# Splitting the last q,k products among the scores, shifting the first block's transposed scores, and respacing the mixer weights and the last row blocks

## The chip, the cores and the metric

The kernel runs on one core of a Trainium2 chip. The metric is the device time of one execution in microseconds (us), as the median of several runs. All matrix work is on TensorE (PE in the profile; PEld is its weight load). VectorE is DVE, ScalarE is ACT, GpSimd is POOL, and SP is the engine whose queue issues most transfers. A `q` behind an engine's name in a row (SPq, ACTq) means its instruction queue, for instance when it issues a DMA.

## The reference

One transformer-like block over S = 2048 rows of D = 576 numbers. A condition vector gives six modulation vectors (scale, shift and gate of two halves).

```
x = A_x
h = layernorm(x) * (1 + ca) + sa
x = x + ga * attention(h)      # 32 heads of 18, causal, window of 256 keys, output projection wo
h = layernorm(x) * (1 + cb) + sb
x = x + gb * mixer(h)          # token shift between gelu(layernorm(h) @ w1) and @ w2,
                               # then an MLP 576 -> 4608 -> 576 (w3, w4), both with residuals
```

All products are carried out to nearly full precision: each operand is split into a high part, rounded to the matmul type, and the rest (low part), and three products (high x high, low x high, high x low) are summed. So a product over 576 = 4 x 128 + 64 input numbers takes 4 x 3 + 2 = 14 matmuls.

## The kernel before, in words

**Phase A** (`phase_a`, L127) does the first half of the block, and its stages overlap:

- *Products.* The rows come in four groups of 512 (g = 0 to 3). `vproj` (L394) makes v; `qproj(m, g)` (L413) makes the m-th set of 128 of the 1152 rows of transposed q and k for group g: 14 matmuls of 128x512 (L422) into one PSUM bank, a high part by ACT (L424), a low part by DVE (L425), and two stores to DRAM (`qkh`, `qkl`, L427), issued on ACT's queue. The PSUM bank comes from `dense` (L387), which takes tag "sc" and tag "st" in turn; each tag has three banks. The order of the products is the list `jobs`; its last seven are (m, g) = (8,1), (7,2), (3,2), (8,2), (7,3), (3,3), (8,3).
- *Attention units.* There are 32 units, each for one group of 512 queries and four heads: n = 0 to 7 belong to g = 0 (the first block, with fewer keys), 8 to 15 to g = 1, and so on. A unit's operands are loaded into one of four buffers U (`uload`, L444; the transfers are at L451), which reuse the memory of the products' inputs and weights. In `s2` (L464) PE makes 16 score tiles (L477, tag "sc"), and DVE takes each one's row maximum (L484), which also frees the bank. The maxima, negated and split (L490, L491), are transposed by PE (`mT`, L498, tag "tr"), copied by ACT (`ms`, L500) and written into the operand U by a DMA (L501, "the ms store"). Then `s3` (L505) makes the scores again, transposed and with the maximum subtracted by the matmul (X, L526, plus a mask by L527, tag "st", three banks), ACT takes the exponential (P, L533), PE multiplies with v (`av`, L548), ACT copies the result (L553), PE transposes it back (`oT`, L560, tag "tr"), DVE divides (L562, L566), and every second unit SP stores the rows (`od`, L570).
- *Row blocks.* For each 128 rows `s4` (L734) loads attention's rows (`or`) and x (`xr`), transposes and splits them (`split9`, L64: PE L68 and L72, ACT L69 and L73, DVE L70 and L74), multiplies with `wo` in two halves (L761) and adds (L762), stores xp, and then normalizes twice in place, each time with a store (L99, L101, the store hbd; L884, the store xnd). L99 overwrites what the store of xp reads. Row blocks 0 to 11 are done in phase A beside the next block's units, 12 to 15 at the start of the next phase.
- *Weights of the mixer.* At the end of phase A `load_w1` (L785) loads w1 in ten pieces (SP, L803 and L77, L78) through two raw buffers, splits them by ACT (L825, L826) and DVE (L827, L829), and `load_w2` (L833) does the same for w2 (SP L842, ACT L857, DVE L858).

**Phase B and C** (`phase_bc`, L869) do the mixer: transposes of the normalized rows (`xnT`, L1055, split by ACT L911 and DVE L912), w1 (L957), w2 (L1010), and the MLP (L1116 and L1145).

**What sets the order.** Each step has a due time in units (one attention unit is 1.0), and `play` (L40) issues steps in order of due time. Phase A is built under a setting that fixes this order on PE, POOL and SP; on ACT and DVE, and in the later phases, the framework's scheduler orders the instructions itself. A product has 3.25/12.5 = 0.26 units. The products end at `t_end`, and the first score is due 1.55 units ahead of that (`u0`), so the last six products lie among scores. A unit that starts at tb has its 16 scores from tb to tb + 0.95 (each maximum is listed a little behind its score), mT at tb + 1.15, X from tb + 1.5 (`o3`) to tb + 2.5, oT at tb + 2.72 and its store at tb + 2.82. The due times of a row block are the seven numbers of `d5`: load, transposes, first half, second half, first and second statistics, and the delay of a store behind the step before it:

```
d5 = (-1.1, 0.0, 0.3, 0.5, 1.3, 2.3, 0.55)
```

Of the kernel before, what the change touches and what calls it, by code (L numbers as in the profile page):

```python
# [8 lines left out]
F32 = mybir.dt.float32  # L9
# [10 lines left out]
P = 128  # L20
# [30 lines left out]
class Kern:  # L51
# [75 lines left out]
    def phase_a(self):  # L127
        nc = self.nc
# [10 lines left out]
        with ExitStack() as st:  # L139
# [86 lines left out]
            def warm(k):  # L226
                def f():
                    pw = self.ps.tile([P, 512], F32, tag="sc", name=f"pw{k}", bufs=self.b_sc)
                    for _ in range(self.n_warm[k]):
                        nc.tensor.matmul(pw, self.zb, self.zb.unsqueeze(1).to_broadcast([P, 4, P]), start=True, stop=True)  # L230
                return f
# [155 lines left out]
            def dense(shape, name):  # L387
                tag, nb = banks_p[turn[0] % len(banks_p)]
                turn[0] += 1
                return self.ps.tile(shape, F32, tag=tag, name=name, bufs=nb)  # L390
# [19 lines left out]
                    nc.scalar.copy(dst, pv.rearrange("p (h d) -> p h d", d=DH))  # L410
                return f

            def qproj(m, g):  # L413
                def f():
                    L, w = hT[g], Wq[m]
                    pq = dense([P, 512], f"pq{m}_{g}")
                    pl = []
                    for k in range(KC):
                        pl += [(w[:, k, :], L[:, k, :]), (w[:, KC + 1 + k, :], L[:, k, :]), (w[:, k, :], L[:, KC + k, :])]
                    pl += [(w[:, KC, :], L[:, 2 * KC, :]), (w[:, 2 * KC + 1, :], L[:, 2 * KC, :])]  # L420
                    for n, (a, b) in enumerate(pl):
                        nc.tensor.matmul(pq, a, b, start=(n == 0), stop=(n == len(pl) - 1))  # L422
                    hl = pp.tile([P, 2, 512], F32R, tag="P", name=f"hl{m}_{g}", bufs=self.b_p)
                    nc.scalar.copy(hl[:, 0, :], pq)  # L424
                    nc.vector.tensor_tensor(out=hl[:, 1, :], in0=pq, in1=hl[:, 0, :].bitcast(F32), op=ALU.subtract)  # L425
                    for n, dst in enumerate((qkh, qkl)):
                        nc.scalar.dma_start(dst[m * P:(m + 1) * P, g * 512:(g + 1) * 512], hl[:, n, :].bitcast(F32))  # L427
                return f
# [194 lines left out]
            s4 = self.s4  # L623

            def sub2(c, g, hq, tb):
                st, f1, f2 = s2(c, g, hq)
                return [(tb + 0.95 * t / 16, f) for t, f in st] + [(tb + 0.96 + 0.06 * self.lt, f1), (tb + 1.05 + self.l_m, f2)]

            def sub3(c, g, hq, tb):
                st, n, f1, f2, f3 = s3(c, g, hq)  # L630
                e = max(t for t, _ in st) / n * self.ww
                return [(tb + self.ww * t / n, f) for t, f in st] + [(tb + e + self.l_f, f1), (tb + e + self.l_f + self.l_o, f2), (tb + e + self.l_f + self.l_o + self.l_s, f3)]

            UN = 12.5
            dv, dq = 1.9 / UN, 3.25 / UN
            T0 = -16.2
            ev = [(T0 - 1.99, lambda: lns[0][0]()), (T0 - 1.98, consts), (T0 - 1.975, cond), (T0 - 1.97, warm(0))]
# [10 lines left out]
            jobs = []  # L648
# [10 lines left out]
                jobs += [("q", m, g) for m in late]  # L659
            T = T0  # L660
            first, last = {}, {}
            for kind, a, b in jobs:
                g = a // 4 if kind == "v" else b
                key = ("v", b) if kind == "v" else ("q", a)
                first.setdefault(("h", g), T)
                first.setdefault(key, T)
                last[key] = T
                if kind == "v":
                    if g == b == 0:
                        ev += [(T0 + 0.001 * (4 * n + a), vproj(a, b, n)) for n in range(3)]  # L670
                    else:
                        ev.append((T, vproj(a, b)))
                    T += dv
                else:
                    ev.append((T, qproj(a, b)))
                    T += dq
            self.t_end = T
            for t in range(4, NT):
                g, i = divmod(t, 4)
                ld, stt, nm, tr = lns[t]  # L680
# [16 lines left out]
            shift = self.t_end + self.u0  # L697

            n = 0
            for g in range(NGA):  # L700
                for c in range(NCH):
                    for hq in range(2):
                        tb = n + shift
                        tu = tb - self.u_ld
                        ev.append((max(tu, ta[n] + 0.01) if n < 4 else tu, uload(c, g, hq)))
                        ev.append((tb - 0.001, lambda c=c, g=g, hq=hq, tb=tb: sub2(c, g, hq, tb)))
                        ev.append((tb + self.o3 - 0.001, lambda c=c, g=g, hq=hq, tb=tb + self.o3: sub3(c, g, hq, tb)))
                        n += 1
                for i in range(4 if g < 3 else 0):
                    t4 = n - 1 + shift + self.o3 + self.ww + self.l_f + self.l_o + self.l_s + self.l_r + 2.0 * i - self.d5[0]  # L710
                    ev += [(t4 + d, f) for d, f in s4(g, i, self.d5)]
            uw = shift + 2.0
            wb, steps = woload()
            ev.append((uw, wb))
# [2 lines left out]
            for v in (2, 3, 4, 5):  # L717
                steps, spill, store = modvec(v)
                t0 = T0 + self.t_mv + self.d_mv * (v - 2)
                for k, (ld, ch) in enumerate(steps):  # L720
                    ev += [(t0 + 0.3 * k, ld), (t0 + 0.3 * k + 0.5, ch)]
                ev += [(t0 + 2.0, spill), (t0 + 2.1, store)]
            tw = n - 0.1 + shift
            wb, steps = self.load_w1()
            ev.append((tw, wb))
            w2 = self.load_w2()
            for n, (ld, f) in enumerate(steps + w2):
                d = 0.17 if n < len(steps) else 0.08
                t0 = tw + 0.17 * min(n, 10) + 0.08 * max(0, n - 10)
                ev += [(t0 + 0.01 if n < 18 else t0 + 1.4 * d - 0.005, ld), (t0 + 1.4 * d, f)]  # L730
            with self.tc.manual_schedule(engines=self.manual):
                play(ev)

# [445 lines left out]
    u0, u_ld = -1.55, 1.3  # L1179
    e_ld, e_tr, e_w2, e_x1, e_lt, e_s4 = 1.2, 0.7, 1.2, 0.8, 0.8, 0.0  # L1180
    d4 = (-0.2, 0.1, 0.38, 0.56, 0.85, 1.2, 0.02)
    d5 = (-1.1, 0.0, 0.3, 0.5, 1.3, 2.3, 0.55)
    l_r = 0.5
    t_mv, d_mv = 3.6, 2.3
# [9 lines left out]
    o3, ww = 1.5, 1.0  # L1194
# [27 lines left out]
```

## Time and profile before

| | before |
|---|---|
| median of three runs | 1772.54 us (1772.39 to 1774.01) |
| the profiled execution | 1772.65 us |
| its span, first to last instruction | 1770.4 us |
| PE busy | 1722.6 us (97%) |
| DVE, ACT, POOL busy | 976.2, 594.3, 389.7 us |
| mean granted TensorE clock | 0.993 |

The profiled execution's time is 2.25 us more than its span. Times in rows are counted from the span's start. In the trace the first score starts at 200.59 us, the last q,k product's matmuls at 222.83, attention's last transposes at 662.64, and the first matmul of w1 at 671.87.

A row of a timeline has the start, the length, the engine, the line, the operation, the tile that it writes and those it reads, the shape and the number of merged instructions; in brackets stands how long the engine was idle before it, and what ended the idle time. A row of the waits has who waited for whom, the sum in us, how often, and the longest.

### The profile page before, as it was taken

The page shows a single profiled execution, that of the slowest core. Times are in us where ns is not written, and L with a number is a line of the kernel's source. Part 1 is how long each engine was busy: PE and PEld are TensorE (multiplying, and loading weights), DVE is VectorE, ACT ScalarE, POOL GpSimd, SP SyncE. Part 2 cuts the span into 40 slices and gives each one's busy share as a digit, 9 for nine tenths or more (in the row PEclk, how much of TensorE's full clock was granted, in tenths as well). Part 3 has the DMA queues.
Part 4 walks back from the last instruction along what each step waited for, and adds up shares of the span by engine and source line. Part 5 has one row for each costly group of instructions (what it writes and reads, how often), then busy time and mean ns, then how long its engine had stood idle before and what let it go on. Part 6 is the DMA issues. An engine that isn't in the chain of part 4 may idle for free.

```text
span 1770.4 us, 30143 instructions
## 1 busy us (share of the span) xinstructions
PE 1722.6 (97%) x11700; PEld 1493.0 (84%) x11700; DVE 976.2 (55%) x2674; ACT 594.3 (34%) x1262; POOL 389.7 (22%) x379
## 2 busy tenths in 40 slices
PE   7999999999999989999999999999999999999999
PEld 5898766777777768899899999999999999999998
DVE  5412378788888866977544444444444444444434
ACT  4622156655555565344211111111111111111111
POOL 4543431000000000211342333224431121122100
PEclk8999999999999999999999999999999999999999
DMA  6536654444544436622211111111110000000002
GB/s 177 148 110 208 200 161 124 117 147 121 153 126 147 129 111 191 201 81 89 63 56 36 49 42 56 34 36 56 56 36 29 16 29 14 29 29 29 1 1 107
DMA packets 97712, 156.89 MB, mean 89 GB/s; under 512 B 11034, under 2 KB 40478, under 8 KB 97570
## 3 DMA queue, kind: packets, MB, share of 16 engines
q1 hardware_dynamic: 86612, 135.12, 25.5%
q10 hardware_dynamic: 10958, 19.85, 3.2%
q8 instruction: 93, 1.52, 0.4%
q14 instruction: 49, 0.40, 0.1%
HBM read 107.06 MB, written 47.20 MB: 87 GB/s over the span
## 4 chain that ended last, share of the span: by engine, by line
PE 55%; DVE 2%; POOL 1%; issue 0%; DMA 0%; SPq 0%; ACT 0%; ACTq 0%; DVEq 0%; POOLq 0%
PE p L1145 26%; PE p L1116 22%; PE p L1118 2%; PE p L1117 2%; PE w L1010 2%; PE pg L957 2%; DVE x L1011 0%; DVE G L975 0%; DVE G L962 0%; DVE LNT L70 0%; DMA r<-in_B_w_dram 0%; POOL CW L1100 0%; DVE xm L884 0%; DVE CW L1095 0%; DVE Gc L1127 0%
## 5 line engine op out<-in xcount | busy, mean ns | idle before, releaser
L1145 PEld LDWEIGHTS p<-CW,Gc 128*128 128x128 f32 x3456 | 473.8, 188 | 16.2 <-DVE Gc L1127 3.7
L1145 PE MATMUL p<-CW,Gc 128*128 128x288 f32 x3456 | 482.0, 295 | 3.4 <-DVE Gc L1127 3.4
L1116 PE MATMUL p<-LNT,CW 128*128 128x512 f32 x1728 | 419.1, 391 | 0.0
L1116 PEld LDWEIGHTS p<-LNT,CW 128*128 128x128 f32 x1728 | 316.3, 188 | 58.8
L1124 ACT ACTIVATE gfc<-p 128x512 f32<-128x512 f32 x144 | 86.2, 599 | 735.6 <-PE p L1118 735.6
L1149 DVE TENSOR_TENSOR acc<-p,acc 128x288 f32<-128x288 f32 x340 | 154.1, 456 | 319.6 <-PE p L1145 316.2
L484 DVE CUSTOM_DVE_ANT_0 sc<-sc,mask 128x384 f32<-128x384 f32 (+2 forms) x512 | 260.5, 556 | 65.9 <-PE sc L477 63.2
L533 ACT ACTIVATE P<-X 128x384 f32<-128x384 f32 x480 | 221.6, 490 | 121.5 <-PE X L527 108.3
L477 PE MATMUL sc<-U 126*128 126x384 f32 (+2 forms) x512 | 195.3, 403 | 7.3 <-DVE m L484 5.6
L526 PE MATMUL X<-U 128*128 128x384 f32 (+2 forms) x704 | 180.8, 316 | 5.9 <-DMA U<-ms 3.2
L1149 DVE TENSOR_TENSOR accw<-p,accw 128x288 f32<-128x288 f32 x204 | 90.0, 453 | 128.5 <-PE p L1145 127.3
L526 PEld LDWEIGHTS X<-U 128*128 128x128 f32 x704 | 127.2, 193 | 34.6 <-issue 24.5
L527 PE MATMUL X<-maskb,identb 128*128 128x256 bf16 x480 | 136.6, 285 | 0.0
L1127 DVE TENSOR_TENSOR Gc<-gfc,Gc 128x512 fp32r<-128x512 f32 x144 | 124.6, 866 | 4.6
L422 PE MATMUL pq<-hT,Wq 128*128 128x512 f32 x504 | 121.3, 397 | 2.4 <-POOL Wq L380 1.6
L422 PEld LDWEIGHTS pq<-hT,Wq 128*128 128x128 f32 x504 | 93.9, 188 | 24.8 <-POOL Wq L380 1.9
L477 PEld LDWEIGHTS sc<-U 126*128 126x128 f32 x512 | 97.7, 197 | 14.3 <-DVE m L484 10.9
L1096 POOL TENSOR_TENSOR CW<-r,CW 128x1024 fp32r<-128x1024 f32 x17 | 41.4, 2436 | 281.7 <-DVE CW L1094 281.7
L548 PE MATMUL av<-P,V 128*32 128x256 f32 (+2 forms) x1472 | 92.4, 381 | 0.0
L1126 ACT CAST Gc<-gfc 128x512 fp32r<-128x512 f32 x144 | 89.5, 622 | 4.6
L1100 POOL TENSOR_TENSOR CW<-r,CW 128x1152 fp32r<-128x1152 f32 x17 | 46.5, 2734 | 157.7 <-DVE CW L1099 157.7
L527 PEld LDWEIGHTS <-identb 128*128 128x128 bf16 x480 | 46.2, 96 | 36.9 <-issue 20.7
(1056 smaller groups left out, 1959.3 us busy)
## 6 DMA issues: line engine op xcount, KB each, us to landing
U<-qkh SPq DMA_DIRECT2D x156, 72.0 KB
U<-qkh SPq DMA_DIRECT2D x96, 108.0 KB
r<-in_B_w_dram SPq DMA_DIRECT2D x18, 576.0 KB
qkh<-hl ACTq DMA_DIRECT2D x36, 256.0 KB
qkl<-hl ACTq DMA_DIRECT2D x36, 256.0 KB
r<-in_B_w_dram SPq DMA_DIRECT2D x18, 512.0 KB
U<-qkl SPq DMA_DIRECT2D x78, 72.0 KB
U<-qkl SPq DMA_DIRECT2D x48, 108.0 KB
```

The costliest lines, as they stand in the source:

```text
L422: nc.tensor.matmul(pq, a, b, start=(n == 0), stop=(n == len(pl) - 1))
L477: nc.tensor.matmul(sc[:, lo:], QZ[:KR, q, i * P:(i + 1) * P], KZ[:KR, j, i * P + lo:(i + 3) * P], start=True, stop=True)
L484: nc.vector.tensor_tensor_reduce(out=sc[:, lo:], in0=sc[:, lo:], in1=mask[:, lo:], scale=1.0, scalar=-3e38, op0=ALU.add, op1=ALU.max, accu ...
L526: nc.tensor.matmul(X[:, x0:x0 + nb, :].rearrange("p a b -> p (a b)"), KZ[:, j, kb * P:(kb + 1) * P], QZ[:, q, qb * P:(qb + nb) * P], start ...
L527: nc.tensor.matmul(X[:, 0::2, :], self.identb, mk, start=False, stop=True)
L533: nc.scalar.activation(Pb[b][:, q, :], Xb[b, q].rearrange("p a b -> p (a b)"), AF.Exp, scale=SCALE)
L548: nc.tensor.matmul(abox[0][32 * q:32 * q + 32, q0:q0 + w], V[4 * g + kb][:, hv:hv + 32], Pb[b][:, q, p0:p0 + w], start=(first and n == 0), ...
L1116: nc.tensor.matmul(pg, W3[:, ws, fs], L[:, xs, :], start=(i == 0), stop=False)
L1126: nc.scalar.copy(Gh, gf)
L1127: nc.vector.tensor_tensor(out=Gl, in0=gf, in1=Gh.bitcast(F32), op=ALU.subtract)
L1145: nc.tensor.matmul(po, a, w, start=(i == 0), stop=(i == len(seq) - 1))
L1149: nc.vector.tensor_tensor(out=acc[t][:, cs], in0=po, in1=acc[t][:, cs], op=ALU.add)
```

## The change

It has four parts.

- The last seven q,k products are each issued in four pieces of 4, 4, 3 and 3 matmuls, 0.065 units apart, instead of one run of 14. Scores that are due in between are issued between the pieces. These products take their bank from tag "st" alone.
- For the units of the first block (g = 0), the transposes of the maxima (mT) and all of `s3` come 0.1 units later. The row blocks of that group keep their times.
- The load of the mixer's weights begins at 30.8 units behind the first score instead of 31.9. The pieces of w1 follow each other by 0.26 units instead of 0.17, and each is split 0.5 units behind its load instead of 0.24; for w2 it is 0.1 instead of 0.08, and 0.19 instead of 0.11.
- Row blocks 8 to 11 (g = 2) are 2.3 units apart instead of 2.0, except the last one: 0.9 units are taken off it, which puts its transposes and projection where they were. Its later steps come sooner (`d6`): its first statistics 0.75 units behind its transposes instead of 1.3, its second 1.1 instead of 2.3, and its stores 0.05 instead of 0.55 behind the step before.

```diff
-            def qproj(m, g):
+            pqs = {}
+
+            def qproj(m, g, part=None):
                 def f():
                     L, w = hT[g], Wq[m]
-                    pq = dense([P, 512], f"pq{m}_{g}")
+                    if part is None:
+                        pq = dense([P, 512], f"pq{m}_{g}")
+                    elif part == 0:
+                        pq = pqs[m, g] = self.ps.tile([P, 512], F32, tag="st", name=f"pq{m}_{g}", bufs=self.b_st)
+                    else:
+                        pq = pqs[m, g]
...
-                    for n, (a, b) in enumerate(pl):
-                        nc.tensor.matmul(pq, a, b, start=(n == 0), stop=(n == len(pl) - 1))
+                    own = range(len(pl)) if part is None else range(*self.q_parts[part:part + 2])
+                    for n in own:
+                        nc.tensor.matmul(pq, *pl[n], start=(n == 0), stop=(n == len(pl) - 1))
+                    if own[-1] < len(pl) - 1:
+                        return
...
-                return [(tb + 0.95 * t / 16, f) for t, f in st] + [(tb + 0.96 + 0.06 * self.lt, f1), (tb + 1.05 + self.l_m, f2)]
+                return [(tb + 0.95 * t / 16, f) for t, f in st] + [(tb + 0.96 + 0.06 * self.lt, f1), (tb + 1.05 + self.l_m + (0 if g else self.l_g0), f2)]
...
-                    ev.append((T, qproj(a, b)))
+                    if len(parts) < self.n_split and (kind, a, b) in jobs[-self.n_split:]:
+                        parts.append(T)
+                        ev += [(T + dq * n / 4, qproj(a, b, n)) for n in range(4)]
+                    else:
+                        ev.append((T, qproj(a, b)))
                     T += dq
...
-                        ev.append((tb + self.o3 - 0.001, lambda c=c, g=g, hq=hq, tb=tb + self.o3: sub3(c, g, hq, tb)))
+                        o3 = self.o3 + (0 if g else self.l_g0)
+                        ev.append((tb + o3 - 0.001, lambda c=c, g=g, hq=hq, tb=tb + o3: sub3(c, g, hq, tb)))
...
-                    t4 = n - 1 + shift + self.o3 + self.ww + self.l_f + self.l_o + self.l_s + self.l_r + 2.0 * i - self.d5[0]
-                    ev += [(t4 + d, f) for d, f in s4(g, i, self.d5)]
+                    t4 = n - 1 + shift + self.o3 + self.ww + self.l_f + self.l_o + self.l_s + self.l_r + (2.0, 2.0, 2.3)[g] * i - self.d5[0] - (0.9 if (g, i) == (2, 3) else 0)
+                    ev += [(t4 + d, f) for d, f in s4(g, i, self.d6 if (g, i) == (2, 3) else self.d5)]
...
-            tw = n - 0.1 + shift
+            tw = n - 1.2 + shift
...
-                d = 0.17 if n < len(steps) else 0.08
-                t0 = tw + 0.17 * min(n, 10) + 0.08 * max(0, n - 10)
-                ev += [(t0 + 0.01 if n < 18 else t0 + 1.4 * d - 0.005, ld), (t0 + 1.4 * d, f)]
+                t0 = tw + 0.26 * min(n, 10) + 0.1 * max(0, n - 10)
+                lag = 0.5 if n < 10 else 0.19
+                ev += [(t0 + 0.01 if n < 18 else t0 + lag - 0.005, ld), (t0 + lag, f)]
...
+    l_g0 = 0.1
+    q_parts, n_split = (0, 4, 8, 11, 14), 7
+    d6 = (-1.1, 0.0, 0.3, 0.5, 0.75, 1.1, 0.05)
```

More of the change, by code (lines that the diff above doesn't have):

```diff
@@ L661, in phase_a @@
             first, last = {}, {}
+            parts = []
             for kind, a, b in jobs:
```

## The prediction

> **What bounds the kernel now.** I read the page first, then busy time by stage, then what TensorE (PE) waited for in each stage, and last the timelines of the two places that the change touches.
>
> ```profile
> span 1770.4 us, 30143 instructions
> PE 1722.6 (97%) x11700; PEld 1493.0 (84%) x11700; DVE 976.2 (55%) x2674; ACT 594.3 (34%) x1262; POOL 389.7 (22%) x379
> ...
> 195.00:227.00 32.00, 28.16 (x123) 21.17 (x121) 14.65 (x56) 5.17 (x9) 6.97 (x5) 1.00 0.55 175
> 227.00:310.00 83.00, 77.76 (x725) 55.81 (x729) 67.54 (x292) 51.05 (x111) 19.97 (x17) 1.00 0.49 143
> 310.00:640.00 330.00, 323.35 (x2899) 244.99 (x2890) 272.81 (x954) 195.29 (x432) 15.86 (x40) 1.00 0.44 131
> 640.00:680.00 40.00, 32.98 (x251) 25.28 (x242) 19.89 (x61) 24.31 (x65) 2.78 (x6) 0.83 0.56 172
> 680.00:870.00 190.00, 180.21 (x1364) 173.48 (x1363) 146.21 (x424) 74.61 (x195) 41.38 (x59) 1.00 0.40 127
> 870.00:1770.00 900.00, 896.71 (x5354) 816.77 (x5352) 391.60 (x756) 170.74 (x280) 208.38 (x108) 1.00 0.12 36
> ```
>
> Each stage row gives its length, then busy time of PE, weight load, DVE, ACT and POOL, granted clock, DMA share and GB/s. PE is busy 97% of the span and is the bound everywhere. The change adds and removes no matmul; it only moves work, so it can pay only in PE's idle time and in time at a lowered clock. The execution took 1772.65 us, 2.25 more than its span and 0.11 over the median of 1772.54; I sum against 1772.65. A measurement of this kernel can tell about 0.2%, or 3.5 us, from no change.
>
> Idle are 3.8 us in 195:227 (the last q,k products among the first scores), 5.2 in 227:310 (first query block), 7.0 in 640:680 (attention's end into the next phase), the last also at a mean clock of 0.83. After 870 PE is never short of work, so what is gained ahead of it should reach the end unless a transfer on the way is late.
>
> **The split q,k products.** What PE waited for in 195:227, then the start of the mixture:
>
> ```profile
> PE sc L477 <- DVE m L484: 2.2, 5, 0.5
> PE pq L422 <- DVE m L484: 0.7, 1, 0.7
> PE sc L477 <- issue: 0.4, 1, 0.4
> PE sc L477 <- DVE hl L425: 0.2, 1, 0.2
> ...
> 195.74 0.27 ACTq L451 DMA_DIRECT2D U<-qkl  x1
> 197.23 3.53 PE L422 MATMUL pq<-hT,Wq 128*128 128x512 f32 x14
> 200.59 0.22 PE L477 MATMUL sc<-U 126*128 126x128 f32 x1
> 201.27 0.33 PE L477 MATMUL sc<-U 126*128 126x128 f32 x1 [0.45 <-DVE m L484]
> ...
> 200.86 0.30 DVE L484 CUSTOM_DVE_ANT_0 sc<-sc,mask 128x128 f32<-128x128 f32 x1 [3.20 <-PE sc L477]
> 211.41 0.57 DVE L484 CUSTOM_DVE_ANT_0 sc<-sc,mask 128x384 f32<-128x384 f32 x1 [2.35 <-PE sc L477]
> ```
>
> A product is 14 matmuls in one run of 3.53 us, so 0.25 each; then a handful of scores comes at once, and the next one waits for DVE's maximum to free a score buffer. In pieces of 4, 4, 3 and 3 there is one score (sometimes two) behind each 0.75 to 1.0 us of products. One maximum takes DVE 0.30 us for 128 columns and 0.57 for 384 (last two rows), so it is done before the next score. The products also leave the score banks for the other three ("st"). So the 2.2 + 0.7 + 0.4 + 0.2 = 3.5 us can go.
>
> Against it: the first score is now behind four matmuls of its neighbour instead of 14, ten matmuls or 2.5 us earlier, at about 198.2. The last load of its operands is issued at 195.74, on ACT's queue. Its landing isn't shown; the nearest row is unit 2's ms store, issued at 243.98 (below), for which PE stops waiting 4.2 us later. By that the load lands at 199.9 and the first score waits 1.7 us; at half that latency it waits nothing. Term: -3.5 + 0.7 = -2.8, bounds -3.5 to -1.8. The ring of three "st" banks replaces six banks: a product has two products' time, about 9 us with their scores, to be evacuated, and no row above names a wait for "st"; cost 0. If ACT fell behind by a product, PE would wait up to that product's 3.5 us.
>
> ```profile
> 234.45 0.64 ACTq L501 DMA_DIRECT2D U<-ms  x1
> 243.98 0.62 ACTq L501 DMA_DIRECT2D U<-ms  x1
> 248.17 0.41 PE L526 MATMUL X<-U 128*128 128x256 f32 x2 [1.33 <-DMA U<-ms]
> ...
> PE mT L498 <- DVE o L566: 1.9, 3, 0.9
> PE X L526 <- DMA U<-ms: 1.7, 2, 1.3
> PE mT L498 <- DVE mr L491: 1.3, 2, 0.7
> ```
>
> **First block 0.1 unit later.** The two stores lie a unit apart, 9.5 us, so 0.1 unit is about 1 us. The last three rows are the waits of 227:310. The transposes of the maxima (mT) wait 1.9 + 1.3 = 3.2 us for DVE. Both mT and the transposed scores X move, so mT stands behind one or two more scores and meets the short, 128-column maxima of the next unit instead of the long ones. Of the 3.2 us, 0.9 is the first unit of the second block, which isn't moved; there the room between oT and mT shrinks by 0.1 unit, at two units. I take -1.5 of the 2.3; bounds -2.3 to +2.0 (two units 1 us each). The distance from mT to X stays 0.35 unit, so the 1.7 us for the ms store stay; 0, bounds -1.7 to +1.
>
> **The end of attention.** PE's waits in 640:680, then stretches of 5 us, then the rows around the longest:
>
> ```profile
> PE X L526 <- ACT P L533: 2.1, 3, 1.6
> PE xnT1pa L1055 <- DVE T L912: 1.8, 1, 1.8
> PE X L526 <- DMA U<-ms: 1.4, 1, 1.4
> ...
> 645.00:650.00 5.00, 3.56 (x33) 2.44 (x26) 3.42 (x10) 3.60 (x10) 0.58 (x2) 0.95 0.51 194
> 650.00:655.00 5.00, 3.37 (x19) 2.65 (x22) 1.90 (x9) 2.12 (x7) 0.51 (x1) 0.50 0.32 86
> 655.00:660.00 5.00, 5.00 (x50) 3.25 (x45) 0.99 (x6) 3.74 (x13) 0.00 (x0) 0.86 0.36 110
> 670.00:675.00 5.00, 4.45 (x19) 3.97 (x20) 2.91 (x9) 2.37 (x7) 0.00 (x0) 0.50 0.92 275
> 675.00:680.00 5.00, 5.00 (x38) 4.96 (x37) 1.93 (x5) 3.81 (x8) 0.00 (x0) 0.81 0.76 250
> ...
> 633.48 1.83 PE L761 MATMUL po<-Wom,oT 128*128 128x288 f32 x12
> 647.65 0.47 PE L526 MATMUL X<-U 128*128 128x128 f32 x2 [1.44 <-DMA U<-ms]
> 653.40 0.69 PE L526 MATMUL X<-U 128*128 128x256 f32 x2 [1.63 <-ACT P L533]
> ...
> 646.41 0.82 DVE L99 SCALAR_TENSOR_TENSOR xr<-xr,b10mv,cb 128x576 f32<-128x576 f32 x1 [4.13 <-DMA xp<-xr]
> 649.81 4.06 SPq L803 DMA_DIRECT2D rw<-in_B_w_dram  x3
> 652.41 0.40 ACT L825 CAST W1m<-rw 128x256 fp32r<-128x256 f32 x1 [2.43 <-DMA rw<-in_B_w_dram]
> 643.68 1.64 ACT L533 ACTIVATE P<-X 128x384 f32<-128x384 f32 x4 [0.31 <-ACT P L533]
> ...
>   DMA rw<-in_B_w_dram: 5.3, 6
> ```
>
> The last unit's X waits 1.44 us for its ms store: no scores are left to fill the time behind mT. In units from the first score, row block 10's transposes move from 31.42 to 27.42 + 2 x 2.3 = 32.02, so its first half of the output projection falls at 32.32, between the last mT (31 + 1.15) and X (31 + 1.5). It is at least 1.83 us of PE work, paid elsewhere before. Term -1.4.
>
> Then a chain of queues: DVE stands 4.13 us at L99 for the xp store; the lower halves of W1 behind it free the two raw buffers late; SP loads W1 at 649.81; ACT stands 2.43 us for that load, with the exponentials behind it; PE waits 1.63 us at 653.40. W1's copies began at 31.9 + 0.24 = 32.14 units, 0.24 behind their loads; now they begin at 30.8 + 0.5 = 31.30 and stand 0.5 unit behind them, 4.8 us instead of 2.3. That covers the 2.43 us. Four copies instead of six remain beside the last X. On SP the loads are moved ahead of row blocks 9 and 10's stores and one attention store (31.82); a load that waits for its buffer holds those up, but they are read only in the next phase. Term -1.6.
>
> Behind the first wait the granted clock is 0.5 until about 656: the three rows lose 0.25 + 2.5 + 0.7 = 3.45 us of full clock, less half of the 1.63 us in which PE waited anyway, 2.6. With neither wait left I count it gone: -2.6. Together -5.6; bounds 0 to -6.1.
>
> The Trainium skill, "TensorE: Matmul & The Clock Gate", Part 1, puts the half clock down to a whole idle window of about 3.4 us. Here a single wait of 1.44 us goes before it, so this trace doesn't bear that length out. By that rule the slow stretch wouldn't come from this wait.
>
> The second slow stretch (670 to 677) follows the entry to the next phase: PE needs one transpose split by ACT and DVE before the next (the 1.8 us). Moved there are row block 11's steps behind its projection, 0.5 to 1.7 units earlier on SP and DVE, and W2 loads, of which five instead of three now stand ahead of the last attention store on SP. The nearest row for a DVE step behind a store, with that split queued after it, is the 4.13 us; a gain would be what row block 11 no longer takes of DVE later. I take 0, bounds -1.5 to +4.1. W1's copies beside the last scores: three sets on a DVE that is 83% busy (272.81 of 330); 0, bounds 0 to +2.
>
> **Sum.** -2.8 - 1.5 - 5.6 = -9.9; 1772.65 - 9.9 = 1762.75, said as 1763.
>
> **The rivals.** *One half only.* The products' gain is eaten by loads that come as late as before (the first score, the ms stores), or the end of attention finds another late step. For it: DMA is 55% busy in 195:227, and PE idles on both DVE and DMA in the same units. Left is about 4.3 or 5.6 us: 1768.4 or 1767.
>
> *The clock stays.* If the slow stretch at 649 doesn't depend on that wait, the 2.6 us stay: 1765.4. For it: the 1.33 us wait at 248.17 left the clock at 1.00 (stage 227:310). Against it: each of the two slow stretches follows a wait of over 1.4 us at once. The rule of the Trainium skill named above would give this case.
>
> *Nothing measurable.* The order on DVE and ACT is the program's scheduler's own, not written by hand, and a new one gives new waits of the old sum: 1769.1 to 1773.
>
> *Slower: the copies stand in ACT's way.* ACT's order isn't held to the planner's times. If W1's copies are put right behind their loads, each of ten stands for its transfer in front of exponentials, now while PE still has scores to do. At 2.43 us each, less the three X buffers' 1.2 us (three exponentials of 0.41, from 1.64 for four), that is 1.2 x 10 = 12 us, and the 1.6 and 2.6 us don't go. 1772.65 - 2.8 - 1.5 - 1.4 + 12 = 1779. It decides once a copy waits longer than 1.2 us at ACT's head. Against it: with less than half the lag ACT stood for these loads six times, 5.3 us in all (last row).
>
> **How the numbers follow.** Forecast 0.50; one half only 0.17, of which 0.04 within 0.2%; clock stays 0.08; nothing measurable 0.13; slower 0.12. Faster by over 0.2%: 0.50 + 0.13 + 0.08 = 0.71; within: 0.04 + 0.13 = 0.17; slower 0.12. The range: at the low end all movable waits go, -3.5 - 2.3 - 6.1 - 1.5 - 1.7 = -15.1, so 1757.5; at the high end the cases up to no change, 1773. That leaves out the slower case and little else.
>
> **What would show it.** Right: in the changed profile the scores' waits for DVE between 195 and 225 below 1 us (before 3.5); mT's waits in the first block below 2 us; no wait over 1 us of the last X; a clock of 1.0 from the last scores to the entry of the next phase; the second slow stretch still there. Wrong: the first score waiting over 1.5 us for its operands; long waits of X for exponentials from the W1 copies on; a second slow stretch longer than 7 us; or a time above 1769.

## The result and the profile after

| | before | changed |
|---|---|---|
| median of the runs compared (6 each) | 1773.28 us (1771.1 to 1777.23) | 1762.87 us (1761.1 to 1767.01) |
| ratio to before, 95% interval | | 0.994 (0.9926 to 0.9954) |
| the profiled execution | 1772.65 us | 1767.01 us |
| its span | 1770.4 us | 1764.9 us |

The change saves 10.4 us; the forecast was 1763 us, 9.9 us less than the profiled run of before. The profiled execution of after is the slowest of its six, so the two profiles are only 5.5 us apart. A second profile of the same changed kernel ("the second profile" below, span 1760.5 us) is 9.9 us shorter than that of before; where the two differ, both are given. In the changed kernel the lines stand lower: L422 is L430, L477 to L570 are ten more, L761 and L762 are L777 and L778, L825 is L841, L912 is L928.

The profile page of after, and its busy time by the stages of the prediction, with two shorter windows (columns as in the prediction):

```profile
span 1764.9 us, 30133 instructions
PE 1719.7 (97%) x11700; PEld 1493.4 (85%) x11700; DVE 978.4 (55%) x2674; ACT 593.6 (34%) x1262; POOL 388.7 (22%) x379
```

```profile
195.00:227.00 32.00, 30.71 (x165) 25.07 (x163) 21.75 (x79) 7.45 (x14) 9.40 (x6) 1.00 0.62 207
227.00:310.00 83.00, 77.95 (x724) 57.15 (x723) 65.96 (x282) 52.41 (x113) 17.44 (x15) 1.00 0.49 141
...
630.00:640.00 10.00, 8.49 (x71) 6.47 (x70) 3.73 (x17) 4.65 (x13) 0.00 (x0) 0.83 0.68 201
640.00:680.00 40.00, 32.93 (x273) 27.19 (x272) 27.39 (x81) 23.86 (x64) 3.36 (x8) 1.00 0.51 163
680.00:870.00 190.00, 181.46 (x1344) 174.68 (x1344) 139.15 (x405) 71.54 (x185) 39.78 (x57) 0.98 0.37 119
845.00:855.00 10.00, 7.21 (x30) 6.61 (x31) 5.09 (x11) 1.54 (x4) 4.19 (x5) 0.66 0.31 92
```

PE's idle time in 195:227 fell from 3.84 to 1.29 us. In 640:680 it did not fall (32.98 busy before, 32.93 now), but the clock there went from 0.83 to 1.00. A shorter slow stretch stands earlier (0.83 over 630:640 is 3.4 us at half clock), and a new one where the MLP begins (0.66 over 845:855 is 6.8 us at half clock).

The waits of PE in 195:227 (one row is all there is), in 227:310 and in 640:680:

```profile
PE X L536 <- DMA U<-ms: 1.2, 1, 1.2
...
PE X L536 <- DMA U<-ms: 2.7, 3, 1.8
PE mT L508 <- DVE o L576: 1.4, 3, 1.1
PE sc L487 <- DVE m L494: 0.7, 1, 0.7
...
PE X L536 <- ACT P L543: 1.6, 1, 1.6
PE xnT1pa L1071 <- DVE T L928: 1.3, 1, 1.3
PE xnT1pb L1073 <- DVE T L932: 1.1, 1, 1.1
```

The waits of scores and products are gone, all 3.5 us (3.1 of them for DVE). In the first block mT's waits fell from 3.2 to 1.4 us, but X's for the ms stores rose from 1.7 to 3.9 us, with the one that the earlier start brings into the first window. At the end of attention the wait for the ms store is gone, and the longest wait for an exponential is as long as before. The timeline of after at these places:

```profile
198.98 0.30 PE L487 MATMUL sc<-U 126*128 126x128 f32 x1
199.12 1.14 PE L430 MATMUL pq<-hT,Wq 128*128 128x512 f32 x4
200.10 0.34 PE L487 MATMUL sc<-U 126*128 126x128 f32 x2
200.27 0.91 PE L430 MATMUL pq<-hT,Wq 128*128 128x512 f32 x3
...
634.31 0.40 ACT L841 CAST W1m<-rw 128x256 fp32r<-128x256 f32 x1 [2.67 <-DMA rw<-in_B_w_dram]
634.62 0.24 ACT L842 CAST W1a<-rw 128x64 fp32r<-128x64 f32 x1
634.76 0.86 ACT L543 ACTIVATE P<-X 128x384 f32<-128x384 f32 x2
...
650.38 0.40 ACT L841 CAST W1t<-rw 128x256 fp32r<-128x256 f32 x1 [2.23 <-DMA rw<-in_B_w_dram]
...
635.30 0.57 PE L536 MATMUL X<-U 128*128 128x384 f32 x1 [1.50 <-ACT P L543]
651.70 0.44 PE L536 MATMUL X<-U 128*128 128x384 f32 x1 [1.60 <-ACT P L543]
```

The first four rows are the pieces of 4 and 3 with one or two scores between, and no bracket: PE waits for nothing. The other rows are the old chain at a new place. ACT stands 2.67 us for a load of W1 with exponentials queued behind it, and PE waits 1.50 us for one of them; 16 us on it happens again (2.23 and 1.60 us). The list of PE's waits names only the middle link, "ACT P"; ACT's own row shows what that engine stood for.

By PE's starts in the two timelines, stage by stage (second profile in brackets): from the start of product (8,1) to the first score of unit 16, 209.35 us before and 204.06 after, -5.3 (-6.0); from there to the first matmul of w1, -2.3 (-2.4); to the first matmul of the MLP, -1.3 (-2.2); to the MLP's thousandth matmul +2.5 (+1.4), at the slow stretch; from there to the end 0.0 (0.0). The starts of (8,1) themselves differ by +0.9 (-0.8), in a part that isn't changed. All together -5.5 (-9.9). So somewhat more than forecast came at the start of attention, and less at its end. The slow stretch where the MLP begins is no cost of the change: each of the thirteen profiles of the other kernels and of the changed one has half clock there, and that of before is the exception. So the two sums by the traces understate the change by 1 us or a little more.

### The profile page after: what moved, and what is told of

It is laid out like the page before. It is cut to its first block, busy times and chain, and to the rows that moved or that the text cites. A ratio compares the mean times of both kernels' runs of the same rounds, so it can differ in the third digit from the quotient of the medians.

```text
span 1764.9 us, 30133 instructions
## 1 busy us (share of the span) xinstructions
PE 1719.7 (97%) x11700; PEld 1493.4 (85%) x11700; DVE 978.4 (55%) x2674; ACT 593.6 (34%) x1262; POOL 388.7 (22%) x379
## 4 chain that ended last, share of the span: by engine, by line
PE 56%; DVE 2%; POOL 0%; issue 0%; DMA 0%; ACT 0%; SPq 0%; ACTq 0%; DVEq 0%; POOLq 0%
PE p L1161 26%; PE p L1132 22%; PE p L1134 2%; PE p L1133 2%; PE w L1026 2%; PE pg L973 2%; DVE x L1027 0%; DMA r<-in_B_w_dram 0%; DVE G L991 0%; POOL CW L1116 0%; DVE LNT L70 0%; DVE CW L1111 0%; DVE xm L900 0%; DVE G L978 0%; DVE Gc L1143 0%
## 5 line engine op out<-in xcount | busy, mean ns | idle before, releaser
L487 PE MATMUL sc<-U 126*128 126x384 f32 (+2 forms) x512 | 199.0, 403 | 4.2 <-DVE m L494 3.5
L430 PE MATMUL pq<-hT,Wq 128*128 128x512 f32 x504 | 123.6, 398 | 1.6 <-POOL Wq L380 1.6
L430 PEld LDWEIGHTS pq<-hT,Wq 128*128 128x128 f32 x504 | 93.3, 188 | 22.5 <-POOL Wq L380 1.9
```

The lines of the kernel that those rows point to most:

```text
L430: nc.tensor.matmul(pq, *pl[n], start=(n == 0), stop=(n == len(pl) - 1))
L487: nc.tensor.matmul(sc[:, lo:], QZ[:KR, q, i * P:(i + 1) * P], KZ[:KR, j, i * P + lo:(i + 3) * P], start=True, stop=True)
```

## The experiments

All were run beside the kernel before; each ratio is to that, with its 95% interval. Diffs are against the changed kernel unless it is said otherwise. "Old weights" and "old row blocks" are these lines of the kernel before:

```diff
# old row blocks
-                    t4 = n - 1 + shift + self.o3 + self.ww + self.l_f + self.l_o + self.l_s + self.l_r + (2.0, 2.0, 2.3)[g] * i - self.d5[0] - (0.9 if (g, i) == (2, 3) else 0)
-                    ev += [(t4 + d, f) for d, f in s4(g, i, self.d6 if (g, i) == (2, 3) else self.d5)]
+                    t4 = n - 1 + shift + self.o3 + self.ww + self.l_f + self.l_o + self.l_s + self.l_r + 2.0 * i - self.d5[0]
+                    ev += [(t4 + d, f) for d, f in s4(g, i, self.d5)]
# old weights
-            tw = n - 1.2 + shift
+            tw = n - 0.1 + shift
-                t0 = tw + 0.26 * min(n, 10) + 0.1 * max(0, n - 10)
-                lag = 0.5 if n < 10 else 0.19
-                ev += [(t0 + 0.01 if n < 18 else t0 + lag - 0.005, ld), (t0 + lag, f)]
+                d = 0.17 if n < len(steps) else 0.08
+                t0 = tw + 0.17 * min(n, 10) + 0.08 * max(0, n - 10)
+                ev += [(t0 + 0.01 if n < 18 else t0 + 1.4 * d - 0.005, ld), (t0 + 1.4 * d, f)]
```

| kernel | us | ratio (95%) |
|---|---|---|
| split products alone | 1766.45 | 0.9959 (0.9946 to 0.9973) |
| shift of the first block alone | 1773.01 | 0.9998 (0.9988 to 1.0008) |
| weights and row blocks alone | 1767.99 | 0.9964 (0.9952 to 0.9977) |
| changed, without the shift | 1759.96 | 0.9919 (0.9905 to 0.9932) |
| the same again | 1761.54 | 0.9934 (0.9922 to 0.9946) |
| changed, again | 1763.44 | 0.9944 (0.9928 to 0.9961) |
| changed, products in one run, banks "st" | 1765.68 | 0.9956 (0.994 to 0.9972) |
| row blocks alone | 1770.69 | 0.9988 (0.9978 to 0.9998) |
| weights alone | 1772.35 | 0.9992 (0.9983 to 1.0) |
| without the shift, X 0.1 later | 1762.95 | 0.9936 (0.9924 to 0.9948) |
| without the shift, four raw buffers | 1765.26 | 0.9955 (0.9943 to 0.9967) |
| without the shift and `d6` | 1766.51 | 0.9958 (0.9946 to 0.997) |

### The parts, one at a time

The split alone (old row blocks, old weights):

```diff
-    l_g0 = 0.1
+    l_g0 = 0.0
```

> Only the last seven q,k products in pieces (bank "st"); no shift of the first block, mixer weights and row blocks as before. Theory A (PE no longer waits for DVE's maxima between 195 and 227 us, and what is gained there reaches the end): 4 to 4.5 us under the kernel before, about 1768.8; the scores' waits for DVE there under 0.5 us instead of 3.5; the end of attention as before, with both slow stretches of the clock. Rival B (the early gain is eaten by loads that come as late as before, and all of the change's 10 us comes from the end of attention): within 1.5 us of before.

Measured: -7.3 us (0.0041 of 1774.47). Its trace has 0.4 and 0.3 us of waits of scores in 195:227, both for DMAs. From (8,1) to unit 16 it takes 202.64 us, 6.7 less than before. The term was -2.8, bounds -3.5 to -1.8: the split is worth more than twice its forecast. The other kernels agree: over the same stretch, with neither mT nor X shifted, the five profiles with the split have 201.92 to 203.75 us, the four without it 209.35 to 210.17.

The shift alone (old row blocks, old weights):

```diff
-    q_parts, n_split = (0, 4, 8, 11, 14), 7
+    q_parts, n_split = (0, 4, 8, 11, 14), 0
```

> Only the shift of the first block's transposed maxima and transposed scores by 0.1 unit. Theory A (it trades mT's waits for DVE against waits at the first X and at the step to the second block): within 1 us of before, mT's waits in 227 to 310 us about 1.5 instead of 3.2 us. Rival B (my prediction's term): 1.5 us faster than before, about 1771.5.

Measured: no difference that can be told; the interval, -2.1 to +1.4 us, holds the forecast's -1.5 as well as 0. PE's waits in 227:310 of this kernel:

```profile
PE X L536 <- DMA U<-ms: 2.1, 3, 1.0
PE mT L508 <- DVE o L576: 1.4, 3, 1.1
```

Before these were 1.7 for X and 3.2 for mT. Only 1.8 of mT's wait went, and 0.4 came back at X. From (8,1) to unit 16 it takes 208.64 us, 0.7 less than before.

The end of attention alone (`l_g0 = 0.0` and `n_split` 0 as in the two diffs above):

> Only the end of attention: mixer weights and row blocks as in the change, products in one run, no shift. Theory A (the ms wait and part of the slow clock go; two waits for exponentials of 1.5 us each stay, because copies of w1 stand at ACT's head): 4 to 6 us under before, 1767 to 1769, with X waiting about 3 us for exponentials and nothing for the last ms store. Rival B (all of the 10 us): 1763 to 1764.

Measured: -6.4 us (0.0036). The size is the forecast's 5.6, but not by its steps. PE's waits in 615:680:

```profile
PE X L536 <- ACT P L543: 2.7, 3, 1.3
PE xnT1pa L1071 <- DVE T L928: 1.3, 1, 1.3
PE xnT1pb L1073 <- DVE T L932: 1.2, 1, 1.2
```

The ms store's 1.4 us are gone; the exponentials' 2.1 us are not (2.7).

All but the shift (diff as in the first experiment, with the new row blocks and weights), run twice:

> The changed kernel without the shift of the first block. Theory A (the shift is worth nothing): the changed kernel's time within 1 us, 1762 to 1764. Rival B (with split products the latencies behind mT get tight and the shift covers them): 1 to 3 us slower than the changed kernel, 1764 to 1766.

> The changed kernel without the shift once more, as the base of the three others of this group. Theory A (the shift costs 2 to 4 us beside split products): ratio 0.991 to 0.9925, 1760 to 1761. Rival B (its first time was chance): 0.994, as the changed kernel twice.

Measured: 0.9919 and 0.9934, the fastest version that was run. The parts add up: 0.0041 + 0.0036 = 0.0077, that is 13.7 us, against 14.4 and 11.7. The changed kernel has 0.9940 and 0.9944 in its two measurements. The means differ by 0.0015, 2.7 us, in favour of leaving the shift out; the intervals overlap or touch, so that is likely and not settled. A gain of the shift shows in none of these times.

By the traces most of this loss does not stand where the shift is. From (8,1) to unit 16 the changed kernel takes 204.06 and 203.35 us, without the shift it is 203.75 and 202.96. From the last score to the first matmul of w1 it takes 36.04 and 36.01 us, against 33.19 and 33.99: there both profiles of the changed kernel have 3.4 us of half clock (from 635 and 634 us on), which neither of the other two has at this place. The kernel of the next section has the shift too, and neither that stretch nor the loss (33.56 us). So it is not shown that the shift itself costs 2.7 us.

> The changed kernel once more, beside the others of this group. Theory A (it pays 2 to 3 us for the shift when the products are split): ratio 0.993 to 0.995. Rival B (the gap to the version without the shift was chance between groups of runs): 0.992, as that version.

The changed kernel again gave 0.9944 beside the first 0.994. Its profile is the second profile of the section before.

### Why the split is worth more: order or banks

The seven products in one run of 14 as before, but from the banks "st" alone:

```diff
-                        ev += [(T + dq * n / 4, qproj(a, b, n)) for n in range(4)]
+                        ev += [(T + dq * n / 4, qproj(a, b, n)) for n in range(1)]
...
-    q_parts, n_split = (0, 4, 8, 11, 14), 7
+    q_parts, n_split = (0, 14), 7
```

> Last seven products in one run of 14 as before, but all from bank tag "st"; no pieces. Shift, weights and row blocks as in the change. Theory A (the pieces make the gain: scores still come in bursts behind 14 matmuls and wait for DVE): at least 4 us slower than the changed kernel, about 1767, with 2 to 3.5 us of waits of scores for DVE between 195 and 227 us. Rival B (the score banks that the products leave free make the gain): within 1 us of the changed kernel.

Measured: 0.9956, 2.2 us slower than the changed kernel beside it, with intervals that overlap. PE's waits in 195:227, then two rows of its timeline:

```profile
PE sc L487 <- DVE m L494: 2.2, 6, 0.5
PE sc L487 <- issue: 0.4, 1, 0.4
PE sc L487 <- DVE hl L435: 0.2, 1, 0.2
```

```profile
201.99 3.41 PE L430 MATMUL pq<-hT,Wq 128*128 128x512 f32 x14
205.23 0.52 PE L487 MATMUL sc<-U 126*128 126x256 f32 x3
```

The handfuls of scores (x3 at once) wait just as before, 2.8 us in all, 2.2 of it for the maxima. But the 0.7 us of a product that waited for a maximum to free its bank are gone, and from (8,1) to the last q,k product's last matmul it takes 30.81 us; before it was 33.08, in the changed kernel 27.56. So of the 5.5 us that this stretch lost, the banks give 2.3 and the pieces 3.2. At the first score of unit 16, with the shift in all of these kernels, it is 2.8 for the banks (205.82 us from (8,1), against 208.64 with the shift alone) and 1.8 to 2.5 for the pieces. Each of these is one or two profiles. The pieces are worth about what the prediction said (2.8). The banks, put at "cost 0", are a gain.

### Which of mT and X should move

Without the shift of mT, X and what follows 0.1 unit later in the first block (on the kernel without the shift):

```diff
-                        o3 = self.o3 + (0 if g else self.l_g0)
+                        o3 = self.o3 + (0 if g else 0.1)
```

> Without the shift of mT, but the transposed scores and all behind them 0.1 unit later in the first block, so that mT and X are 0.45 unit apart instead of 0.35. Theory A (the first block waits about 2.5 us for ms stores, and 1 us more room takes most of it): 1 to 2 us under the version without the shift. Rival B (what counts is the crowded step to the second block, where the last X of the first block meet the first X of the second): 1 to 3 us over it.

Measured: 0.9936 beside 0.9934 for the kernel without it: nothing. PE's waits in 227:310, here and in the kernel without the shift:

```profile
PE mT L508 <- DVE o L576: 2.6, 3, 1.1
PE X L536 <- DMA U<-ms: 1.8, 3, 0.6
PE sc L487 <- DMA U<-qkl: 0.9, 1, 0.9
PE sc L487 <- DVE o L576: 0.3, 1, 0.3
```

```profile
PE mT L508 <- DVE o L576: 1.9, 3, 0.9
PE X L536 <- DMA U<-ms: 1.4, 2, 1.0
PE mT L508 <- DVE mr L501: 1.1, 1, 1.1
```

Three ways to set mT and X, and the waits of the first block are 5.6, 4.4 and, in the changed kernel, 4.8 us. Two profiles of one kernel differ as much: the first of the kernel without the shift has 5.8. They are traded among DVE, the ms store and the operands' loads, and hardly fall.

### Weights and row blocks apart

Row blocks alone (old weights, no split, no shift), then weights alone (old row blocks, no split, no shift):

> Only the row blocks respaced; weights as before, products in one run, no shift. Theory A (row block 10's projection fills the time of the last ms store and takes the first slow stretch away): 3 to 4 us under before, no wait of the last X for its ms store. Rival B (the early weights carry it): under 1.5 us.

> Only the mixer weights' load earlier and wider; row blocks as before, products in one run, no shift. Theory A (the copies still stand at ACT's head for their loads, as in the changed kernel's profile): 0 to 2 us under before, the 1.4 us wait for the last ms store still there and X still waiting over 1 us for exponentials. Rival B (my prediction's term: that wait of 1.6 us goes and with it the slow stretch): 3 to 4 us under before.

Measured: -2.1 and -1.4 us (0.0012 and 0.0008), 3.5 together, where both in one kernel give 6.4. The intervals of the three are some 2 us to each side, so that the two give more together is likely and not settled. In each the ms store's wait at the end of attention is gone already, so either suffices for that. PE's wait for one DVE step in 680:870 stands out, first with the row blocks alone, then with the weights alone; with both (the kernel of the third experiment) it is 0.7 us (two waits, the longer 0.5):

```profile
PE po L777 <- DVE xr L778: 2.3, 1, 2.3
```

```profile
PE po L777 <- DVE xr L778: 2.4, 1, 2.4
```

Without `d6`, that is, row block 11 with the step times of the others (on the kernel without the shift):

```diff
-                    ev += [(t4 + d, f) for d, f in s4(g, i, self.d6 if (g, i) == (2, 3) else self.d5)]
+                    ev += [(t4 + d, f) for d, f in s4(g, i, self.d5)]
```

> The version without the shift, with row block 11's later steps at their old distances. Theory A (its steps then fall into the entry of the next phase, where DVE is the last to be waited for; that is why weights and row blocks together give more than the sum of each alone): 2 to 3 us slower than the version without the shift, with longer waits for DVE between 660 and 740 us. Rival B (it was off the path): within 1 us.

Measured: 0.9958 beside 0.9934, 4.3 us slower by the ratios. PE's waits in 680:870 and its timeline at the longest, then busy time in a window there:

```profile
PE po L777 <- DVE xr L778: 3.0, 2, 2.8
```

```profile
715.57 2.67 PE L777 MATMUL po<-Wom,oT 128*128 128x288 f32 x11 [2.81 <-DVE xr L778]
```

```profile
714.00:720.00 6.00, 4.43 (x22) 4.44 (x23) 4.92 (x19) 0.00 (x0) 0.79 (x2) 0.72 0.29 96
```

PE stops for 2.81 us where DVE has to free the projection's bank. The kernel with `d6` also stops there, 1.19 us at a transpose one step ahead and 0.25 at the projection; the stop there is half as long, and the clock stays at 1.00. Here it is at half for 3.4 us ((1 - 0.72) x 6 = 1.7 us lost). From the first matmul of w1 to the first of the MLP it takes 160.52 us, against 158.52. So the trace shows 2.0 us, and the two profiles differ by 1.9 from (8,1) to the end; the 4.3 of the medians is more, and the two intervals touch; the profiled execution, 1763.06 us, is the fastest of its five. That row block 11's early steps help by having its DVE steps out of the way at this place is the reading that fits. But the row blocks alone have them too and still wait 2.3 us, so `d6` is not enough by itself: it takes the weights' new times as well, and which order of DVE steps comes out of both is the scheduler's.

### The copies of W1 in front of the exponentials

Four raw buffers for w1 instead of two, and its loads 0.43 unit earlier, the copies where they were (on the kernel without the shift):

```diff
...
-                ev += [(t0 + 0.01 if n < 18 else t0 + lag - 0.005, ld), (t0 + lag, f)]
+                ev += [(t0 - 0.42 if n < 10 else t0 + 0.01 if n < 18 else t0 + lag - 0.005, ld), (t0 + lag, f)]
...
-                raw = raws[k, z] = self.rp.tile([P, 288], F32, tag="wraw", name=f"rw1{k}_{z}", bufs=2)
+                raw = raws[k, z] = (self.pp if z else self.rp).tile([P, 288], F32, tag="wr" if z else "wraw", name=f"rw1{k}_{z}", bufs=2)
```

> The version without the shift, with four raw buffers for w1 instead of two (two of them those of the q,k weights, which are free by then) and each load 0.43 unit earlier. Theory A (exponentials wait because a copy of w1 at ACT's head waits for its load): X's waits for exponentials at the end of attention, 1.5 to 3 us, fall under 0.5, and the time is 1 to 3 us lower. Rival B (the copies themselves, or the order the scheduler picks, take ACT's time): no change within 1 us.

Measured: 0.9955, 3.7 us slower than the kernel without the shift beside it; the intervals overlap slightly, but none of its six times is below the highest of the other's five. ACT's standing for loads of w1 in 615:680 fell from 6.6 us to 1.4. PE's waits in 615:680, of this kernel and of the one beside it:

```profile
PE sc L487 <- DVE m L494: 2.6, 4, 1.0
...
PE X L536 <- ACT P L543: 0.7, 1, 0.7
```

```profile
PE X L536 <- ACT P L543: 2.1, 2, 1.5
```

What was to be shown is shown: with the loads there in time, PE's wait for exponentials falls from 2.1 to 0.7 us. But with their data there earlier, the scheduler put the copies earlier too, among the last scores: in 621 to 629 us the lower halves of W1 stand between DVE's maxima, the scores wait 2.6 us for maxima in all (1.9 of it in this stretch), and the last score starts at 629.95 instead of 626.57. Later the projection waits 3.0 us for DVE at L778, where the kernel beside it waits 0.7. The gain was paid back twice.

## Why the prediction was right, step by step

The time came out (1762.87 for 1763) with the sign, the size and the bound right. But the terms erred in both directions, and their errors cancelled: that the sum lies 0.1 us off is luck.

**The split products, -2.8.** Right in mechanism, mis-sized. All 3.5 us of waits went. The first score came 5.4 us behind the start of (8,1) in the profile shown, where before it was 7.8, so 2.5 us earlier as forecast; it stands at 198.98 instead of 198.2 because (8,1) itself starts 0.9 us later. It waited for its load between 0 (profile shown) and 1.0 us (kernel without the shift), for the 0.7 taken. The term measured alone was -7.3 us by the runs, -6.7 by the trace. Two things were missing in it. "Cost 0" for the ring of three "st" banks was too small: the products' leaving the score banks gave 2.3 us by itself. The row "PE pq <- DVE m" (0.7 us) had shown that a product can be stuck behind a maximum; that a product in its turn holds a score bank for its 3.5 us and its evacuation is the likely rest, which no run separates. And a stop of PE costs more than its idle time: from (8,1) to the last matmul of the last q,k product, PE idled 3.5 us less (33.08 us with 29.59 busy before, 27.56 with 27.52 after), but the stretch is 5.5 us shorter. Before, a 128-column score that stands alone is 0.22 to 0.33 us long in its row; after, the next piece starts 0.17 us behind the start of two such scores (200.10 and 200.27 in the timeline above). Those ends are modelled, so this reading fits and is not more.

**The first block 0.1 later, -1.5.** This step was not borne out. Alone it measured -0.4 us, with the forecast still inside the interval, and -0.7 by the trace up to unit 16; beside the split the kernel with it is more likely 2.7 us slower, for the most part at another place. mT's waits fell as said (3.2 to 1.4 us; the profile was to show below 2), but "the distance from mT to X stays 0.35 unit, so the 1.7 us for the ms store stay" did not hold: they became 3.9 with the split, 2.1 without. What mT no longer waits for DVE, X in part waits for the store: the chain from the maxima over mT, ACT and the DMA to X was the limit, not the place of mT in it. That last is argued from the sums of the waits; no run changed the store's latency.

**The end of attention, -5.6.** It measured -6.4 alone, but two of its three steps were not as told. The ms store's wait (-1.4) went, as said. The exponentials' wait (-1.6) did not; in 615:680 of after it is 3.3 us, where it was 2.1: "0.5 unit covers the 2.43 us" took the lag that the planner asks for, while on ACT the scheduler sets the order, and there the copies still stand 2.67 and 2.23 us at the queue's head. That is the mechanism of the slower rival. It was not its price: ten such waits of 2.43 us were put there, and four came (5.1 and 2.2 us together in 615:680 of after); before there were six of 5.3 us. The clock's 2.6 us went in part: the long stretch at 649 is gone, one of 3.4 us stands at 635 instead. What made up for it came from the entry to the next phase, for which 0 was taken with bounds -1.5 to +4.1. From the first w1 matmul to the MLP the change gained 1.3 and 2.2 us, and its end of attention alone 2.4 us, past that bound; taking only `d6` out costs 1.9 us by the trace and 4.3 by the medians.

**The rivals.** "One half only" did not come: both halves did. "The clock stays" is undecided, since the stretches move from one execution to the next (see the last section): the profile shown has clock 1.00 in 640:680, against "the second slow stretch still there", while the second profile of the same kernel has it back:

```profile
655.00:670.00 15.00, 12.39 (x77) 11.48 (x76) 11.10 (x30) 6.60 (x16) 2.34 (x6) 0.77 0.79 240
```

(1 - 0.77) x 15 is 3.4 us lost at most, so 6.9 us at half clock. "Nothing measurable" named a danger that is real, a new order with new waits of the old sum: it is what happened to the shift, and to the four raw buffers.

**What was to be seen.** Of the five signs named, the scores' waits for DVE (below 1 us) and mT's (below 2) came. "No wait over 1 us of the last X" did not: 1.60. Nor did "a clock of 1.0 from the last scores": 0.83 over 630:640. The second slow stretch is in one profile of the two. Of the signs against, long waits of X for exponentials behind W1's copies came, twice.

## What to carry to other kernels

A long accumulation that shares its banks with short tiles costs twice, by the tiles that pile up behind it and by the bank that it holds; issue it in pieces, and from another ring. Read a wait on an exponential or a copy back by one more link, to what that engine's own queue stood for, before you count on a lag written into a plan that this engine does not follow. Parts of a respacing should be measured apart and together: here one of the four parts showed no gain that could be told and the kernel without it was the fastest, while the time of the other parts came in part from places that the sum had put at 0.

## What the runs showed of the hardware

The half-clock stretches were not where long idle times alone would put them. The same wait at the MLP's start (PE p for DVE) is 3.4 us in every profile. Busy time around it, in the kernel before and in the two runs of the kernel without the shift, with a row for the end of attention of the latter two:

```profile
840.00:860.00 20.00, 16.16 (x98) 14.11 (x97) 13.65 (x25) 3.95 (x9) 10.03 (x8) 1.00 0.33 101
```

```profile
600.00:680.00 80.00, 72.45 (x621) 57.05 (x620) 58.48 (x194) 48.52 (x125) 6.00 (x14) 1.00 0.47 145
840.00:860.00 20.00, 17.00 (x96) 15.47 (x97) 9.84 (x20) 4.21 (x9) 8.28 (x7) 0.91 0.27 79
```

```profile
600.00:680.00 80.00, 73.61 (x614) 58.65 (x614) 57.87 (x190) 48.66 (x125) 5.89 (x14) 0.96 0.47 144
840.00:860.00 20.00, 16.57 (x93) 14.75 (x92) 9.10 (x19) 4.64 (x10) 8.89 (x7) 0.91 0.31 91
```

Before, it left the clock at 1.00; without the shift 3.4 us of half clock stand beside it ((1 - 0.91) x 20 = 1.8 lost), in the profile shown 6.8. Waits of 1.4 to 1.6 us, on the other hand, have half clock next to them at attention's end, in some profiles and not in others: the last two blocks are one and the same kernel, at 1.00 and 0.96. By the trace's clock records each stretch that ends within the span lasts 3.41 or 6.83 us and nothing else, and the stretches at full clock between them are whole numbers of 3.413 us too. The Trainium skill, "TensorE: Matmul & The Clock Gate", Part 1, has a window of 3413 ns that runs freely, not tied to the kernel. The lengths agree with that, and a phase that differs from run to run would let the same wait fall differently.

The fourteen traces bear this out. Cut each, from 60 to 1700 us, into windows of 3.413 us that begin where its clock records change, and take those at full clock by PE's busy share. All 28 windows with PE busy below 48.3% are followed by half clock, and none of the 6613 with more than 65%; of the 43 between, 10 are. The wait of 3.4 us before fell across two windows, each about half busy (1.72 and 1.67 of 3.41 us), and the clock stayed:

```profile
850.93:854.34 3.41, 1.72 (x10) 1.32 (x8) 0.09 (x1) 1.22 (x2) 3.20 (x3) 1.00 0.66 195
854.34:857.75 3.41, 1.67 (x13) 1.67 (x14) 3.21 (x7) 0.01 (x1) 0.41 (x1) 1.00 0.59 173
```

In the thirteen other profiles one window there has PE busy for at most 28%. In the same way the wait of 1.50 us ahead of the stretch at 635 in the profile shown lies in one window, busy at 56%, while one of 1.47 us in the second profile without the shift is spread over two, at 76 and 81%, and leaves the clock alone. The page's condition of an idle window does not fit the stretch at 635; here the measurement decides: PE idle for more than 52% of a window was enough each time, and at that stretch 44% was. What decides between 48 and 65% busy stays open.

Half clock also costs less than it looks where PE waits anyway: of the two profiles above the second has 6.8 us more of it (3.4 us of full clock), and from the first score of unit 16 to the end takes 1.6 us longer.
